# Folding batch 1's first DFT in four slabs, and moving the stage that fills the wait before the last DFT

## The chip, the cores and the metric

The kernel runs on one core of a Trainium2 chip. The metric is the device time of one execution, in microseconds (us). Engines are named as in the profile: PE is TensorE (PEld its weight loads), DVE VectorE, ACT ScalarE, POOL GpSimd, SP SyncE, which here issues most of the DMAs.

## The reference

```python
def _attn_ref(x, filt_r, filt_i):              # x: (8, 3008, 256) f32
    X = np.fft.rfft(x, axis=1)
    Y = X * (filt_r + 1j * filt_i)[None, :, :]
    return np.fft.irfft(Y, n=x.shape[1], axis=1)

def _moe_ref(x, w_gate, w_val, w_out):         # 24064 tokens, 256 -> 1536 -> 256
    gate = np.maximum(x @ w_gate, 0.0)
    return (gate * (x @ w_val)) @ w_out
```

A filter along the sequence through a real FFT of length 3008 for each of eight batches, then a gated MLP on all tokens.

## The kernel before

3008 is 94 x 32, so each batch goes through four steps of matmuls. **A** is the DFT over the 94 rows n1, in f32, one slab of columns at a time; its result goes to DRAM (Abuf) and comes back with other rows on the partitions. **B** is the transform over the 32 n2 (psX), the product with the filter (tt, uu), and its inverse (psD); **D** is what B leaves: it is copied out of PSUM into dsb by ACT and stored to DRAM (Dbuf). **C** reads it back (dC) and makes the inverse DFT over n1 (psY), which gives the MLP its input. The MLP is a loop of 47 blocks of 512 tokens with 12 steps each (psV, psG, then psO of the block before). Batch 0's A, B and first C stand ahead of the loop. Batches 1 to 7 are mixed inside it, but batch 1's A doesn't fit there: it must be back from DRAM by step 16 or so of the loop, and its x must be there early. So it stands ahead of the loop too, partly inside batch 0's B, partly in the wait for D's way through DRAM to C.

The parts that matter, from the kernel before (cuts are marked with `...`):

```python
def load_x(b, eng, cols):                   # x in pieces of 32 rows, on every 4th partition of all 128
    for c, c0, c1 in cols:
        for m in range(3):
            rows = min(32, B * N1 - (b * N1 + 32 * m))
            eng.dma_start(XF[c][m:m + 4 * rows - 3:4, c0:c1],
                          _ap(x, (b * N1 + 32 * m) * N2 * D + c * w + c0, [[N2 * D, rows], [1, c1 - c0]]))

def items_a(b):                             # A: 16 f32 matmuls of 128 x 96 over 512 columns
        ...
        nc.tensor.matmul(psA[0:NROW], WA, XF[c * NC2 // NX2][:, o:o + 512], start=True, stop=True)
        nc.scalar.copy(st["asb"][:NROW, j * 512:(j + 1) * 512], psA[0:NROW])
        ...                                 # after every fourth: store to Abuf

def first_b(amid):                          # batch 0's B
    for i in range(6):
        fwd(0, i)                           # psX
        if i > 1:
            inv(0, i - 2, cuts=cuts)        # psD, its copies to dsb, the store
        ...                                 # filter products on DVE, some on GpSimd
        amid(i)                             # from the third on: one or two of batch 1's A
    inv(0, 4, cuts=cuts); amid(6); inv(0, 5, cuts=cuts)
...
load_x(1, nc.sync, ((0, 0, 2 * q), (0, 2 * q, 4 * q), (1, 0, 4 * q)))
load_vg(0, DFF // 2)                        # half of the V and G weights
first_b(amid)
load_d(0, 0, 2)                             # dC <- Dbuf, for C
for c in range(2, 4):
    load_vg(c * DFF // 4, (c + 1) * DFF // 4)
load_at(1, 0)
for i, f in enumerate(early):               # the rest of batch 1's A, ten matmuls
    f()
    if i == 5: load_at(1, 1)
    if i == 7:
        for h in range(2): item_c(0, h)     # C of the first block; the last two of A stand behind it
...                                         # the loop; load_at(1, 2), load_at(1, 3) in its first two steps
```

## Time and profile before

| | before |
|---|---|
| median of the first three runs | 902.18 us (902.16 to 902.97) |
| span of the profiled run | 895.9 us |
| TensorE busy | 98% |
| first forward product of batch 0 (psX) | 35.12 us |
| load of C's data issued (D has landed) | 54.70 us |
| C | 58.56 us |
| first MLP matmul (psV) | 60.80 us |
| batch 1's first forward product | 79.67 us, no wait before it |

The prediction shows the page's busy line, the windows by stage, the chain that ended last and TensorE's timeline around C, and how they are read. TensorE's timeline around batch 1's first forward product (start and length in us, engine, line, operation, output and inputs, shapes; a bracket at the end would name a wait):

```profile
79.05 0.60 PE L486 MATMUL psO<-WoT,prod 128*128 128x256 bf16 x4
79.67 0.41 PE L364 MATMUL psX<-at,F 64*64 64x256 bf16 x8
80.02 0.61 PE L467 MATMUL psV<-yT,WvT 128*128 128x512 bf16 x2
```

In the text below, times are often given **after psX0**, the first forward product of batch 0 in that same run, because the stages ahead of it, which the change hardly touches, vary by up to 2 us from run to run. D's landing is read from the moment at which SP issues the first load of C's data, since that issue waits for D's last store.

### The profile page before, as it was taken

What the parts mean: (1) busy time and instruction counts of PE and PEld (TensorE: products, weight loads), DVE (VectorE), ACT (ScalarE), POOL (GpSimd) and SP (SyncE); (2) the same over time, 40 slices, a digit from 0 to 9 for tenths busy, and PEclk for the clock granted to TensorE, in tenths of its full rate; (3) what the DMA queues carried; (4) which work ended last, traced back from release to release, by engine and by line L of the source; (5) the groups of instructions that cost most, each with busy time, mean ns of one, the idle gap of its engine ahead of it and who ended that gap; (6) DMA issues with size and microseconds to landing.
All of it is one profiled execution on the core that took longest, in us unless ns stands there. A gap on an engine that the chain in (4) does not pass through costs nothing.

```text
span 895.9 us, 19186 instructions
## 1 busy us (share of the span) xinstructions
PE 881.8 (98%) x7206; PEld 510.3 (57%) x7206; DVE 569.3 (64%) x873; ACT 499.4 (56%) x891; POOL 363.6 (41%) x361
## 2 busy tenths in 40 slices
PE   7899999999999999999999999999999999999998
PEld 2335555566556665556655666555655566666665
DVE  2636865577665776567766677657766577655553
ACT  3475565556555556555655565555565556555553
POOL 4351399138661376415672167801868000000001
PEclk9999999999999999999999999999999999999999
DMA  9998448534465435463375433763346512241111
GB/s 247 287 230 168 108 141 185 124 82 116 124 155 130 115 104 137 129 139 98 99 176 130 99 101 105 181 133 85 111 139 154 117 32 82 67 88 36 37 30 54
DMA packets 114098, 109.17 MB, mean 122 GB/s; under 512 B 20359, under 2 KB 98599, under 8 KB 113366
## 3 DMA queue, kind: packets, MB, share of 16 engines
q1 hardware_dynamic: 90294, 80.10, 34.6%
q0 software_dynamic: 22992, 26.41, 12.4%
q10 hardware_dynamic: 720, 1.45, 0.4%
q8 instruction: 56, 0.92, 0.4%
q14 instruction: 36, 0.29, 0.1%
HBM read 61.93 MB, written 49.81 MB: 125 GB/s over the span
## 4 chain that ended last, share of the span: by engine, by line
PE 84%; POOL 6%; issue 4%; DMA 3%; DVE 1%; ACT 1%; SPq 0%; POOLq 0%; DVEq 0%
PE psV L467 25%; PE psO L486 25%; PE psG L467 24%; PE psF L323 3%; PE psY L451 2%; PE psD L394 2%; PE psX L364 1%; DMA Fti<-in_filt_i_dram 1%; POOL XP L296 1%; POOL fold L309 1%; POOL XP L310 1%; POOL XP L605 1%; DMA Dbuf<-dsb 1%; PE psJ L520 1%; POOL XP L300 1%
## 5 line engine op out<-in xcount | busy, mean ns | idle before, releaser
L472 DVE SCALAR_TENSOR_TENSOR prod<-psG,vsb 128x512 bf16<-128x512 f32 x564 | 389.2, 690 | 265.9 <-ACT vsb L470 259.1
L470 ACT CAST vsb<-psV 128x512 bf16<-128x512 f32 x564 | 332.1, 589 | 266.1 <-PE psV L467 226.9
L467 PE MATMUL psV<-yT,WvT 128*128 128x512 bf16 x1128 | 336.4, 379 | 0.3 <-ACT vsb L470 0.3
L486 PE MATMUL psO<-WoT,prod 128*128 128x256 bf16 x2256 | 336.4, 273 | 0.0
L467 PE MATMUL psG<-yT,WgT 128*128 128x512 bf16 x1128 | 335.3, 379 | 0.8 <-ACT dsb L401 0.3
L486 PEld LDWEIGHTS <-prod 128*128 128x128 bf16 x2256 | 220.6, 98 | 143.4
L467 PEld LDWEIGHTS <-WgT 128*128 128x128 bf16 x1128 | 110.0, 98 | 135.8 <-issue 2.4
L467 PEld LDWEIGHTS <-WvT 128*128 128x128 bf16 x1128 | 98.4, 98 | 42.1 <-issue 30.8
L258 POOL CAST scr<-yT 128x8 f32<-128x8 bf16 x25 | 4.7, 190 | 263.4 <-ACT yT L456 263.4
L509 POOL DMA_DIRECT2D out_dram<-osb x5 | 2.6, 536 | 196.1 <-ACT osb L499 196.1
L380 DVE TENSOR_TENSOR tt<-psX,Ftr 128x512 bf16<-128x512 f32 x96 | 65.1, 683 | 7.4 <-PE psX L364 7.4
L499 ACT COPY osb<-psO 128x512 f32<-128x512 f32 x92 | 53.9, 586 | 27.4 <-PE psO L486 25.7
L309 POOL TENSOR_TENSOR fold<-XP 128x1024 f32<-128x1024 f32 x24 | 56.5, 2355 | 21.5 <-PE psF L323 20.4
L380 DVE TENSOR_TENSOR uu<-psX,Fti 128x512 bf16<-128x512 f32 x89 | 60.6, 681 | 0.0
L401 ACT CAST dsb<-psD 128x512 bf16<-128x512 f32 x96 | 51.5, 589 | 12.4 <-PE psD L394 12.2
L296 POOL DMA_DIRECT2D XP<-in_x_dram x96 | 56.7, 596 | 1.6 <-issue 0.8
L310 POOL TENSOR_TENSOR XP<-XP 128x1024 f32<-128x1024 f32 x24 | 56.3, 2348 | 1.9
L330 DVE CAST asb<-psF 128x512 bf16<-128x512 f32 x48 | 30.9, 686 | 19.2 <-PE psF L323 14.1
L330 ACT CAST asb<-psF 128x512 bf16<-128x512 f32 x48 | 25.8, 589 | 29.0 <-PE psF L323 29.0
L456 ACT CAST yT<-psY 128x512 bf16<-128x512 f32 x47 | 27.6, 586 | 24.9 <-PE psY L451 24.7
L458 DVE CAST yT<-psY 128x512 bf16<-128x512 f32 x47 | 32.0, 681 | 9.7 <-PE psY L451 9.7
L451 PE MATMUL psY<-M,dC 96*128 96x94 bf16 (+18 forms) x604 | 37.5, 198 | 0.5 <-DMA dC<-Dbuf 0.4
(69 smaller groups left out, 508.2 us busy)
## 6 DMA issues: line engine op xcount, KB each, us to landing
at<-Abuf SPq DMA_DIRECT2D x32, 384.0 KB
dC<-Dbuf SPq DMA_DIRECT2D x64, 192.0 KB
XP<-in_x_dram POOLq DMA_DIRECT2D x48, 256.0 KB, 6.0
Dbuf<-dsb SPq DMA_DIRECT2D x23, 512.0 KB
XP<-in_x_dram POOLq DMA_DIRECT2D x96, 96.0 KB, 2.7
Abuf<-asb SPq DMA_DIRECT2D x96, 96.0 KB
out_dram<-osb SPq DMA_DIRECT2D x69, 94.0 KB
XF<-in_x_dram SPq DMA_DIRECT2D x15, 256.0 KB
```

The lines of the kernel that those rows point to most:

```text
L296: nc.gpsimd.dma_start(xp[r:r + 24, 0:4:2, :], _ap(x, (b * N1 * N2 + o) * D, [[N2 * D, 24], [47 * N2 * D, 2], [1, 512]]))
L309: tt(t, xp[:, 0:2], xp[:, 2:4], op=ALU.add)
L310: tt(xp[:, 2:4], xp[:, 0:2], xp[:, 2:4], op=ALU.subtract)
L330: copy(asf[:, :, q, :], banks[q])
L380: nc.vector.tensor_tensor(p, psX, filt, op=ALU.mult)
L401: nc.scalar.copy(dsb[:, a, o:o + 2, :], psD[a])
L451: nc.tensor.matmul(psY[:, o:o + w], dCs[b, n2 // 8][:, n2 % 8, h * 128:(h + 1) * 128], M1[:, n1:n1 + w], start=True, stop=True)
L467: nc.tensor.matmul(pt[:, :W], w[:, h, ft * 128:(ft + 1) * 128], yt[:, h, :], start=(h == 0), stop=(h == 1))
L470: nc.scalar.copy(vsb, psV[:, :W])
L472: nc.vector.scalar_tensor_tensor(prod, in0=psG[:, :W], scalar=0.0, in1=vsb, op0=ALU.max, op1=ALU.mult)
L486: nc.tensor.matmul(psO[:, t % 2], prods[ft][:, t * 128:(t + 1) * 128], WoT[:, ft, :], start=(ft == 0), stop=(ft == NFT - 1))
L499: copy(osb[:, t0 % 2:t % 2 + 1], psO[:, t0 % 2:t % 2 + 1])
```

## The change

The intent is to shorten the first B and to bring C forward. Batch 1's A leaves the first B. It is done with half the multiplications: the rows n1 and n1 + 47 are first added and subtracted (`fold_half`), and then 64 x 64 tiles do four products at a time (in the kernel before, one f32 matmul of 512 columns takes 0.86). Two slabs of it fill the wait for C, with junk matmuls (their results are never read) between them, meant to keep TensorE's clock up (it was 0.59 and 0.55 from 40 to 44 us in the kernel before); the third follows C, and the fourth goes into the loop at step 4. For these tiles, two on each half of the partitions, x is loaded in pieces that each lie in one half of the partitions. D's last piece gets a buffer of its own, the banks of psX and psD are fixed, and of the V and G weights one quarter, not two, is asked for ahead of the first B.

The core of the diff, cut at `...`:

```diff
+    def load_halves(c):
+        for t in range(3):
+            for h in range(2):
+                nc.sync.dma_start(X1[c][64 * h + t:64 * h + t + 61:4],
+                                  _ap(x, ((N1 + 16 * t) * N2 + 16 * h + 8 * c) * D,
+                                      [[N2 * D, 16], [47 * N2 * D, 2], [1, 8 * D]]))
+    def fold_half(j, eng):
...
+        eng.tensor_tensor(t, xp[:, 0], xp[:, 1], op=ALU.add)
+        eng.tensor_tensor(xp[:, 1], xp[:, 0], xp[:, 1], op=ALU.subtract)
+    def halves_a(j):
...
+        for q in range(2):
+            for h in range(2):
+                for e in range(2):
+                    nc.tensor.matmul(banks[2 * h + q][64 * e:64 * e + 64],
+                                     W1[64 * h:64 * h + 64, 64 * e:64 * e + 64], fold[1, j][e][...],
+                                     start=True, stop=True, tile_position=(64 * h, 64 * e))
...                                          # copies to asb; every second slab: eight stores to Abuf
-    def fwd(b, i):
+    def fwd(b, i, junks=False):
...
+            for _ in range(2 * junks):
+                nc.tensor.matmul(psXs[b, i, e], junk[:, 0:128], junk, start=True, stop=True)
...
-            dsbs[b] = i, sb.tile([128, 2, 4, D], BF16, tag="dsb", bufs=3, name="dsb")
+            pool, bufs = (sb, 3) if b or i < 5 else (pro, 1)
+            dsbs[b] = i, pool.tile([128, 2, 4, D], BF16, tag="dsb", bufs=bufs, name="dsb")
...
-    load_x(1, nc.sync, ((0, 0, 2 * q), (0, 2 * q, 4 * q), (1, 0, 4 * q)))
+    for c in range(2):
+        load_halves(c)
-    load_vg(0, DFF // 2)
-    first_b(amid)
+    load_vg(0, DFF // 4)
+    first_b()
     load_d(0, 0, 2)
+    for j in range(3):
+        fold_half(j, nc.vector)
-    for c in range(2, 4):
+    for c in range(1, 4):
         load_vg(c * DFF // 4, (c + 1) * DFF // 4)
-    load_at(1, 0)
-    for i, f in enumerate(early):
...
+    fold_half(3, nc.gpsimd)
     load_o()
+    warm(6)
+    for j in range(2):
+        halves_a(j)
+        warm((4, 6)[j])
+    for h in range(2):
+        item_c(0, h)
+    halves_a(2)
...
         if b == 1:
-            for c in range(2, 4):
-                at_step(c - 2, lambda c=c: load_at(1, c))
+            at_step(4, lambda: halves_a(3))
+            for c in (0, 2, 1, 3):
+                at_step(4, lambda c=c: load_at(1, c))
```

More of the change, by code (lines that the diff above doesn't have):

```diff
@@ L105, in _tables @@
     fold = np.zeros((128, 4, 32))
+    half1 = np.zeros((128, 4, 32))
     i = np.arange(24)
@@ L115, in _tables @@
             fold[32 * q:32 * q + 24, 2 * odd + 1, 0:24] = np.where(k1 % 47 == 0, 0.0, -np.sin(th))
+        th = 2 * np.pi * (np.outer(np.arange(47) - 23, k1) % N1) / N1
+        for h in range(2):
+            n = np.arange(47)
+            rows = 64 * h + 4 * (n % 16) + n // 16
+            half1[rows, 2 * odd, 0:24] = np.cos(th)
+            half1[rows, 2 * odd + 1, 0:24] = np.where(k1 % 47 == 0, 0.0, -np.sin(th))
     tab = np.concatenate([perm, swap, own.reshape(128, -1), m1], 1)
-    return wa.astype(np.float32), fold.reshape(128, 128).astype(np.float32), f2.astype(NBF16), tab.astype(NBF16)
+    fold = np.stack([fold, half1], 1).reshape(128, 256)
+    return wa.astype(np.float32), fold.astype(np.float32), f2.astype(NBF16), tab.astype(NBF16)
 @with_exitstack
@@ L155 @@
     Dbuf = [dram.tile([NROW * N2, D], BF16, name=f"Dbuf{b}") for b in range(B)]
-    XF = [pro.tile([128, NX2 * D], FP32, name=f"XF{c}") for c in range(N2 // NX2)]
+    XF = [consts.tile([128, NX2 * D], FP32, name=f"XF{c}") for c in range(N2 // NX2)]
+    XD = [t[:, :].rearrange("p (k n) -> p k n", k=4) for t in XF]
+    XP = [XD[j // 2][:, :, 512 * (j % 2):512 * (j % 2) + 512] for j in range(4)]
     WA = pro.tile([128, NROW], FP32)
-    WF = consts.tile([128, 4, 32], FP32)
+    WFS = consts.tile([128, 2, 4, 32], FP32)
+    WF, W1 = WFS[:, 0], WFS[:, 1].rearrange("p c k -> p (c k)")
     M1 = consts.tile([NROW, N1], BF16)
@@ L182 @@
     FILT = ((filt_r, Ftr), (filt_i, Fti))
+    junk = pro.tile([128, 512], BF16, tag="junk", bufs=1)
     tabs = pro.tile([128, tab_h.shape[1]], BF16, tag="tabs", bufs=1)
@@ L261, with fft_tag @@
     turn = {"tags": ("fft", "psv", "psg", "pso"), "i": 0}
-    def fft_tag(side=False):
-        if side and turn.get("side"):
-            return turn["side"]
+    def fft_tag():
         turn["i"] += 1
@@ L273, in one @@
                 st["asb"] = sb.tile([128, NC2 * D], BF16, tag="asb", bufs=4, name="asb")
-            psA = ps.tile([128, 512], FP32, tag=fft_tag(True), name="psA")
+            psA = ps.tile([128, 512], FP32, tag=fft_tag(), name="psA")
             o = (c * NC2 % NX2) * D + j * 512
@@ L280, in one @@
             if j == 3:
-                eng = nc.scalar if b and c > 1 else nc.sync
-                eng.dma_start(_ap(Abuf[b], c * NROW * NC2 * D, [[NC2 * D, NROW], [1, NC2 * D]]),
+                nc.sync.dma_start(_ap(Abuf[b], c * NROW * NC2 * D, [[NC2 * D, NROW], [1, NC2 * D]]),
                                   st["asb"][:NROW])
@@ L306, in fold_chunk @@
         xp = XP[j]
-        t = fs.tile([128, 2, 512], FP32, tag="fold", bufs=2, name="fold")
+        t = sb.tile([128, 2, 512], FP32, tag="fold", bufs=2, name="fold")
         tt = nc.gpsimd.tensor_tensor
@@ L325, in tiled_a, with store_a @@
                                  tile_position=(r, 32 * c))
+        store_a(b, j, banks, (nc.scalar.copy, nc.vector.tensor_copy) * 2)
+    def store_a(b, j, banks, copies):
         asf = sb.tile([128, NC2 * D], BF16, tag="asb", bufs=4, name="asb")
@@ L328, in tiled_a @@
         for q in range(4):
-            copy = nc.scalar.copy if q % 2 == 0 else nc.vector.tensor_copy
-            copy(asf[:, :, q, :], banks[q])
+            copies[q](asf[:, :, q, :], banks[q])
         for c in range(4):
@@ L342, in load_at_tiled @@
                                   [[D, 32], [N2 * D, 24], [1, D]]))
-    POOL_U = ((0, 1), (1, 0), (1, 1), (2, 0), (2, 1), (3, 1), (4, 0))
+    X1 = [t[:, :].rearrange("p (k n) -> p k n", k=2) for t in XF]
+    slabs = {}
+    def load_halves(c):
[4 more added lines that the diff above has]
+                                      [[N2 * D, 16], [47 * N2 * D, 2], [1, 8 * D]]))
@@ new lines, in fold_half @@
+    def fold_half(j, eng):
+        xp = X1[j // 2][:, :, 4 * D * (j % 2):4 * D * (j % 2) + 4 * D]
+        pool, tag = (pro, "half") if j < 2 else (sb, "fold")
+        t = pool.tile([128, 2, 2 * D], FP32, tag=tag, bufs=2, name="half")
+        t = t.rearrange("p q n -> p (q n)")
+        eng.tensor_tensor(t, xp[:, 0], xp[:, 1], op=ALU.add)
+        eng.tensor_tensor(xp[:, 1], xp[:, 0], xp[:, 1], op=ALU.subtract)
+        fold[1, j] = (t, xp[:, 1])
+    def halves_a(j):
+        banks = [ps.tile([128, 2 * D], FP32, tag=t, name="psF") for t in ("psv", "psg", "fft", "fft")]
+        c, m = divmod(j, 2)
+        for q in range(2):
+            for h in range(2):
+                for e in range(2):
+                    nc.tensor.matmul(banks[2 * h + q][64 * e:64 * e + 64],
+                                     W1[64 * h:64 * h + 64, 64 * e:64 * e + 64],
+                                     fold[1, j][e][64 * h:64 * h + 64, 2 * D * q:2 * D * q + 2 * D],
+                                     start=True, stop=True, tile_position=(64 * h, 64 * e))
+        copies = (nc.scalar.copy,) * 4 if j < 3 else (nc.scalar.copy, nc.vector.tensor_copy) * 2
+        for h in range(2):
+            if m == 0:
+                slabs[h] = sb.tile([128, NC2 * D], BF16, tag="asb", bufs=4, name="asb")
+            for q in range(2):
+                o = (4 * m + 2 * q) * D
+                copies[2 * h + q](slabs[h][:, o:o + 2 * D], banks[2 * h + q])
+            if m == 1:
+                for t in range(4):
+                    r = 2 - 2 * (t // 2) + t % 2
+                    nc.sync.dma_start(_ap(Abuf[1], ((2 * h + c) * NROW + r) * NC2 * D,
+                                          [[4 * NC2 * D, 24], [1, NC2 * D]]),
+                                      slabs[h][32 * t:32 * t + 24])
@@ L345 @@
+    POOL_U = ((0, 1), (1, 0), (1, 1), (2, 1), (3, 0), (3, 1), (4, 0))
     ats = {}
@@ L354 @@
     CUTS = (0, 2, 4, 6)
-    def fwd(b, i):
+    def fwd(b, i, junks=False):
         for e in range(2):
-            psXs[b, i, e] = ps.tile([128, 2, D], FP32, tag=fft_tag(), name="psX")
+            tag = "fft" if b or not e else "psv"
+            psXs[b, i, e] = ps.tile([128, 2, D], FP32, tag=tag, name="psX")
+            for _ in range(2 * junks):
+                nc.tensor.matmul(psXs[b, i, e], junk[:, 0:128], junk, start=True, stop=True)
         for m in range(2):
@@ L381, in product, with inv @@
         tus[b, i, e, k] = p
-    def inv(b, i, tags=None, cuts=CUTS):
+    def inv(b, i, tags, cuts=CUTS):
         if i in cuts:
-            dsbs[b] = i, sb.tile([128, 2, 4, D], BF16, tag="dsb", bufs=3, name="dsb")
+            pool, bufs = (sb, 3) if b or i < 5 else (pro, 1)
+            dsbs[b] = i, pool.tile([128, 2, 4, D], BF16, tag="dsb", bufs=bufs, name="dsb")
         i0, dsb = dsbs[b]
-        psD = [ps.tile([128, 2, D], FP32, tag=tags[a] if tags else fft_tag(), name="psD")
+        psD = [ps.tile([128, 2, D], FP32, tag=tags[a], name="psD")
                for a in range(2)]
@@ L404, in inv, with first_b @@
                               dsb[:, :, :o + 2, :])
-    def first_b(amid):
-        cuts = (0, 2, 4, 5, 6)
+    def first_b():
+        cuts, tags = (0, 2, 4, 5, 6), ("psg", "pso")
         for i in range(6):
-            fwd(0, i)
+            fwd(0, i, True)
             if i > 1:
-                inv(0, i - 2, cuts=cuts)
+                inv(0, i - 2, tags, cuts)
             for e in range(2):
@@ L415, in first_b @@
                 product(0, i, e, 1, pool=(i, e) in POOL_U)
-            amid(i)
-        inv(0, 4, cuts=cuts)
-        amid(6)
-        inv(0, 5, cuts=cuts)
+        for i in range(4, 6):
+            inv(0, i, tags, cuts)
     dCs = {}
@@ L511, in o_part @@
                                           osb[o + c0:o + c1, tt % 2])
-    junk = pro.tile([128, 512], BF16, tag="junk", bufs=1)
     def warm(n, cols=512):
-        psJ = ps.tile([128, 512], FP32, tag=fft_tag(True), name="psJ")
+        psJ = ps.tile([128, 512], FP32, tag=fft_tag(), name="psJ")
         for i in range(n):
@@ L535 @@
     load_x(0, nc.sync, ((0, 0, q), (0, q, 2 * q), (0, 2 * q, 4 * q), (1, 0, 2 * q), (1, 2 * q, 4 * q)))
-    nc.sync.dma_start(WF, nc.inline_tensor(fold_h, name="dft_fold").ap())
+    nc.sync.dma_start(WFS, nc.inline_tensor(fold_h, name="dft_fold").ap())
     for (src, dst) in FILT:
@@ L566 @@
         warm(2)
-    load_x(1, nc.sync, ((0, 0, 2 * q), (0, 2 * q, 4 * q), (1, 0, 4 * q)))
-    early = items_a(1)
-    def amid(i):
-        if i < 2:
-            warm(4, 256)
-        else:
-            for _ in range((1, 1, 2, 1, 1)[i - 2]):
-                next(early)()
+    for c in range(2):
+        load_halves(c)
     hold_gpsimd(ats[0][0:32, NG - 1, 0:8])
-    load_vg(0, DFF // 2)
-    turn["tags"], turn["side"] = ("fft", "psv", "psg"), "pso"
-    first_b(amid)
-    turn["tags"], turn["side"] = ("fft", "psv", "psg", "pso"), None
+    load_vg(0, DFF // 4)
+    first_b()
     load_d(0, 0, 2)
+    for j in range(3):
+        fold_half(j, nc.vector)
     nc.gpsimd.dma_start(pro.tile([1, D], BF16, tag="last", bufs=1, name="last"),
                         _ap(Dbuf[0], (N2 * NROW - 1) * D, [[D, 1], [1, D]]))
-    for c in range(2, 4):
+    for c in range(1, 4):
         load_vg(c * DFF // 4, (c + 1) * DFF // 4)
-    load_at(1, 0)
-    for i, f in enumerate(early):
-        f()
-        if i == 5:
-            load_at(1, 1)
-        if i == 7:
-            for h in range(2):
-                item_c(0, h)
-    hold_gpsimd(yTs[0][:, 0, 0:8])
-    load_o()
+    fold_half(3, nc.gpsimd)
+    load_o()
+    warm(6)
+    for j in range(2):
+        halves_a(j)
+        warm((4, 6)[j])
+    for h in range(2):
+        item_c(0, h)
+    halves_a(2)
     prologue.close()
     fs = ctx.enter_context(tc.tile_pool(name="fs", bufs=2))
-    XP = []
-    def clear_chunks():
-        for i in range(4):
-            XP.append(fs.tile([128, 4, 512], FP32, tag=f"XP{i}", bufs=1, name=f"XP{i}"))
-            nc.gpsimd.memset(XP[i], 0.0)
     turn["tags"] = ("fft",)
@@ L615 @@
     C_AT = (8, 10)
-    at_step(2, clear_chunks)
     for b in range(1, B):
```

## The prediction

> **What bounds the kernel now.** I read the page's busy table first, then the windows by stage, the chain that ended last around the start, and TensorE's timeline. Columns of a window: length, then busy time (and instructions) of PE, PEld, DVE, ACT, POOL, then granted clock, DMA share, GB/s.
>
> ```profile
> PE 881.8 (98%) x7206; PEld 510.3 (57%) x7206; DVE 569.3 (64%) x873; ACT 499.4 (56%) x891; POOL 363.6 (41%) x361
> ```
> ```profile
> 28.00:62.00 34.00, 31.27 (x231) 13.10 (x230) 15.21 (x27) 19.94 (x37) 15.39 (x19) 0.95 0.87 249
> 62.00:74.00 12.00, 11.43 (x62) 5.13 (x60) 8.80 (x13) 7.90 (x14) 6.48 (x4) 1.00 1.18 250
> ...
> 160.00:270.00 110.00, 110.00 (x963) 64.19 (x939) 73.53 (x113) 63.14 (x114) 54.62 (x52) 1.00 0.48 122
> ```
> From 160 us on TensorE has no gap, and the change touches nothing in its order there: batches 2 to 7 still fold and transform as before. So the change can act only between the first transform (35.1 us) and batch 1's first forward product (79.67 us). All else is a constant, and the question is by how much that second point moves.
>
> ```profile
> 42.88 0.96 ACT dsb L401 x2
> ...
> 51.16 1.07 ACT dsb L401 x2
> 52.24 0.03 ACT asb L279
> 52.26 2.42 DMA Dbuf<-dsb
> 54.68 0.02 issue
> 54.70 0.33 SPq L427
> 55.02 0.05 issue
> 55.08 3.35 DMA dC<-Dbuf
> 58.42 0.14 issue
> 58.56 0.62 PE psY L451 x12
> 59.18 1.80 PE psA L276 x4
> ```
> ```profile
> 49.42 1.10 PE L276 MATMUL psA<-XF,WA 128*96 128x512 f32 x2
> ...
> 51.01 7.11 PE L276 MATMUL psA<-XF,WA 128*96 128x512 f32 x16
> 58.56 0.62 PE L451 MATMUL psY<-M,dC 96*128 96x94 bf16 x12 [0.43 <-DMA dC<-Dbuf]
> 59.02 1.94 PE L276 MATMUL psA<-XF,WA 128*96 128x512 f32 x4
> 60.80 0.59 PE L467 MATMUL psV<-yT,WvT 128*128 128x512 bf16 x2
> ```
> The reader is to see two chains of nearly the same length: the last copy out of D (52.23) through the store, the load and C (6.33 us from copy to C), and TensorE's own A of batch 1, which fills that wait down to 0.43 us. Each f32 matmul of 512 columns is two records, 0.86 us together (7.11 us for eight matmuls with their drain). The loop starts at 60.80.
>
> ```profile
> 40.00:42.00 2.00, 2.00 (x16) 0.43 (x16) 0.09 (x1) 2.00 (x5) 2.00 (x3) 0.59 1.08 350
> 42.00:44.00 2.00, 2.00 (x18) 0.98 (x15) 1.79 (x3) 1.52 (x4) 1.79 (x2) 0.55 1.14 407
> ```
> Here TensorE has a little over half its clock, right after 34 to 40 us, in which it idled 2.3 us.
>
> [...] 16 f32 matmuls of 24x32 over 512 columns take 1.07 us in the chain, where one alone streams 0.86. [...]
>
> **The change part by part.**
> Removed: sixteen f32 matmuls of A, 16 x 0.86 = 13.8 us of TensorE, six of them inside the first B. Each also had an ACT copy of 0.58. GpSimd's four memsets (7.1 us) go; they lay beside the loop.
> Added: A as four slabs of eight 64x64 tiles. Four tiles run at once, so a slab is 2 x 0.86 + about 0.25 fill = 2.0 us, 8.0 us in all. Junk matmuls: 24 in the first B and 16 in three warm groups, 0.213 each, 8.5 us. TensorE's sum hardly changes; what matters is where it falls.
>
> First B. Before it ran 35.1 to 51.05, since A's matmuls (at half clock at first) stood between its steps. I list the new order with the old durations: DVE product pitch 0.60, ACT copy pitch 0.5 to 0.59, GpSimd product 1.13, eight psX matmuls 0.41, sixteen psD 0.5, four junk 0.85. GpSimd's first product still ends at 39.31, which starts the first inverse; the third GpSimd product frees the second inverse at 41.6; transform 4 is ready 43.35, transform 5 at 45.2; GpSimd's seventh product ends about 47.2, DVE's last 47.75. The last inverse ends about 48.35, and ACT's last copy 49.85: 2.4 us earlier than 52.23. The separate buffer for the last piece only keeps this free: before, the first store had landed at 48.42, well ahead of the last copy (51.16).
>
> D to C. With the same 6.33 us, the data for C are there at 56.2. TensorE comes later, though. DVE's first fold can only start after its last product[...]. Slab 0 then runs to 52.2. The next warm group takes a bank that ACT's third copy of the slab frees at about 53.3, so slab 1 runs 54.15 to 56.1 and six junk matmuls end at 57.4. C runs at 57.4 (58.56 before), a gain of 1.2. After C stands a slab of 2.0 where 1.80 stood, so the loop starts at about 60.0, a gain of 0.8. Its first steps wait for ACT and DVE some 0.6 us as before (0.28 and 0.3 are named in the waits).
>
> In the loop. Slab 3 stands after step 4. TensorE has no slack there (block 0 runs a step in 0.866, four pairs of 0.216), so it costs its 2.0 us in full, and about 0.1 for bank turns. From loop start to batch 1's first transform it was 79.67 - 60.80 = 18.87; it becomes 21.0. So that transform comes at 60.0 + 21.0 = 81.0, against 79.67: 1.3 us later.
>
> Transfers. The quarters of V and G leave the queue free during the first B, but three of them follow D instead of two. From 52 us on some 6.6 MB have to move before 81 us (dC 0.8 + 0.8, weights 1.2 + 0.8, A's store 1.5 and load 1.5); at the 250 GB/s of the windows that is 26.4 us, ending about 79 to 80. A's load follows slab 3's store, so it is just in time; I allow 0 to 1 us.
> Sum on the path: -1.2 (C earlier) + 0.2 (slab 2) + 2.1 (slab 3 in the loop) + 0.2 (transfers) = +1.3, so 903.5.
>
> **The rivals.**
> First: C is bound by its data, not by my warm groups. That a warm group stands just ahead of C speaks for it: whoever placed it seems to have seen TensorE wait there. If fold and banks cost less than I reckon, C runs at 56.2, and the sum is about +0.1. If the first B is also 1 us shorter[...], -1: 901 to 902.
> Second: batch 1's load or the weights come late. The DMA share above 1.1 in 62 to 74 us speaks for it[...]. TensorE would stand still for 1 to 3 us: 904.5 to 906.
> Third: TensorE falls to half clock again in the first B or between the slabs, some 3 us of it: +1 to +1.5. [...]
> Fourth: a loss of everything, a tie at 902, if gain and slab 3 cancel.
>
> **Range and chances.** My steps say 903.5; the first rival, which the placing of the warm groups supports, pulls to 901.5. I weigh them six to four and take 902.7. The range 900.0 to 905.5 holds both and a stall of some 2 us. Two per cent are 18 us, more than the whole stage between first B and loop could give: faster 0.01, same 0.98, slower 0.01.
>
> **What would show it.** Last copy out of D near 49.9; [...] slabs of 2.0 us on TensorE; C at 56.2 to 57.5; first psV near 60; batch 1's first psX near 81 with little wait on its load; from there to the end the same length as before. It is wrong if slabs don't run four tiles at once (3.5 us each), if C comes before 55, or if TensorE waits over 2 us in the loop.

Measured in the kernel after, the folds took 1.21 to 1.23 us each. For three other figures: the junk matmuls of the kernel before stand 0.216 us apart (30 in 6.64 us, the last of them 0.38 long) for the 0.213 reckoned with; the 1.07 us of 16 f32 matmuls of 24x32 is that of their 32 records in the chain, at 240.48 us for one; and the clock of the kernel before is 0.50 in each half microsecond from 40.5 to 43.5 us, and some 3 us of this is what the third rival means by "again".

## The result, and the profile after

The changed kernel took 901.82 us in the median of four runs (901.12 to 904.52); the kernel before, on the same occasion, 902.17 (901.29 to 902.97). The ratio is 1.0002, with a 95% interval from 0.9978 to 1.0026: the same. Ratios in this document are the mean time of one kernel's fast runs over that of the other's fast runs of the same rounds, so not quite the ratio of the medians that are quoted. The outputs of both kernels, and of every experiment below, are correct.

The page's busy line of the kernel after (busy time, share of the span, instructions):

```profile
PE 876.7 (97%) x7146; PEld 510.7 (57%) x7270; DVE 577.7 (64%) x881; ACT 498.0 (55%) x889; POOL 363.6 (40%) x360
```

Its windows by stage, with the columns that the prediction explains:

```profile
28.00:62.00 34.00, 29.33 (x276) 12.16 (x278) 23.34 (x34) 17.28 (x33) 15.71 (x18) 1.00 0.92 232
62.00:74.00 12.00, 11.44 (x63) 4.72 (x64) 7.43 (x12) 8.72 (x16) 5.01 (x4) 1.00 1.23 231
...
160.00:270.00 110.00, 109.10 (x924) 64.59 (x939) 72.74 (x112) 62.47 (x112) 60.86 (x57) 1.00 0.49 126
```

The late stage is as before. In the stage from 28 to 62 us the clock is whole (1.00 where it was 0.95), the DMA engines are busier (0.92 for 0.87), and yet they move less (232 GB/s for 249). The chain of work that ended last, in the kernel after (start, length, what):

```profile
49.64 1.10 ACT dsb L463 x2
50.76 4.49 DMA Dbuf<-dsb
...
55.76 3.40 DMA dC<-Dbuf
...
59.29 0.62 PE psY L511 x12
59.91 1.88 PE psF L384 x16
...
71.21 4.65 DMA Abuf<-asb
...
75.92 7.17 DMA at<-Abuf
83.10 2.29 issue
85.39 0.41 PE psX L425 x8
```

Two things are new in it. D's last store takes 4.49 us, where it took 2.42 before. And the way of batch 1's A through DRAM (its store, its load at<-Abuf) now ends the idle time before psX; before, psX stood behind plain MLP work. TensorE's timeline at the same places:

```profile
57.13 1.47 PE L578 MATMUL psJ<-junk 128*128 128x512 bf16 x6
59.29 0.62 PE L511 MATMUL psY<-M,dC 96*128 96x94 bf16 x12 [0.69 <-DMA dC<-Dbuf]
61.73 0.60 PE L527 MATMUL psV<-yT,WvT 128*128 128x512 bf16 x2
85.39 0.41 PE L425 MATMUL psX<-at,F 64*64 64x256 bf16 x8 [2.79 <-issue]
```

The brackets show that C waited 0.69 us for its data, in spite of the junk ahead of it, and that psX of batch 1 stood still for 2.79 us. For this second wait the profile names no releaser: "issue" is time for which it shows no cause. One piece of batch 1's load is seen to land at 83.10, 2.29 us before psX starts. That the rest of the wait is for the load's other pieces is inferred: the share of the DMA engines was 1.20 from 84.0 to 84.5 us and 0.39 from 85.25 to 85.5, so they ran empty just as psX began. Below, "the wait for batch 1's load" is meant in this sense. Right behind that idle time two windows of the kernel after lie at a little over half clock (the seventh value behind the length, 0.57 and 0.58):

```profile
86.00:88.00 2.00, 2.00 (x9) 1.06 (x8) 1.29 (x3) 0.59 (x1) 0.00 (x0) 0.57 0.04 11
88.00:90.00 2.00, 2.00 (x8) 0.89 (x7) 0.73 (x2) 1.17 (x2) 0.00 (x0) 0.58 0.04 10
```

The timelines of ACT and DVE in the kernel after show the end of the first B and the folds:

```profile
47.54 3.20 ACT L463 CAST dsb<-psD 128x512 bf16<-128x512 f32 x6 [0.96 <-PE psD L456]
48.59 1.21 DVE L373 TENSOR_TENSOR half<-XF 128x1024 f32<-128x1024 f32 x1
49.84 1.23 DVE L374 TENSOR_TENSOR XF<-XF 128x1024 f32<-128x1024 f32 x1
```

The last copy out of D ends at 50.74 us, which is 14.7 after psX0 (52.23 - 35.12 = 17.1 before). So the first B did become 2.4 us shorter. D, however, landed no earlier. The milestones in us after psX0, from one profiled run each; the last but one column is TensorE's wait right before batch 1's first psX:

| run | D landed | C | loop starts | batch 1's psX | wait there | span |
|---|---|---|---|---|---|---|
| before | 19.6 | 23.4 | 25.7 | 44.6 | 0 | 895.9 |
| before, again | 19.1 | 23.1 | 25.3 | 44.1 | 0 | 896.7 |
| after | 19.3 | 23.2 | 25.7 | 49.3 | 2.8 | 902.7 |
| after, again | 18.7 | 23.2 | 25.6 | 48.2 | 1.8 | 900.3 |
| after, a third time | 19.5 | 23.4 | 25.9 | 48.1 | 1.4 | 899.5 |

From batch 1's psX to the end it is 816.2 us before and 817.3 after, of which about 2 are the half clock just shown (an estimate: 4 us at 0.57 and 0.58); in the repeated runs it is 816.6 for before and 816.6 and 816.2 for after. So nearly everything happens where the prediction placed it, between psX0 and batch 1's psX.

### The profile page after: what moved, and what is told of

Its sections match the earlier page's. It is cut to its first block, busy times and chain, and to the rows that moved or that the text cites. A ratio compares the mean times of both kernels' runs of the same rounds, so it can differ in the third digit from the quotient of the medians.

```text
span 902.7 us, 19221 instructions
## 1 busy us (share of the span) xinstructions
PE 876.7 (97%) x7146; PEld 510.7 (57%) x7270; DVE 577.7 (64%) x881; ACT 498.0 (55%) x889; POOL 363.6 (40%) x360
## 4 chain that ended last, share of the span: by engine, by line
PE 85%; DVE 4%; ACT 3%; DMA 3%; issue 2%; SPq 1%; POOL 1%; ACTq 0%; POOLq 0%
PE psG L527 26%; PE psO L546 25%; PE psV L527 24%; DVE prod L532 4%; PE psF L332 3%; ACT vsb L530 3%; PE psD L456 2%; PE psX L425 2%; PE psY L511 1%; DMA XF<-in_x_dram 1%; SPq L187 1%; PE psJ L578 1%; POOL uu L439 1%; DMA at<-Abuf 1%; DMA Abuf<-asb 1%
## 5 line engine op out<-in xcount | busy, mean ns | idle before, releaser
L527 PE MATMUL psG<-yT,WgT 128*128 128x512 bf16 x1106 | 331.4, 380 | 6.4 <-ACT dsb L463 0.6
L527 PE MATMUL psV<-yT,WvT 128*128 128x512 bf16 x1030 | 315.7, 380 | 0.4 <-ACT vsb L530 0.3
L318 POOL TENSOR_TENSOR fold<-XF 128x1024 f32<-128x1024 f32 x24 | 56.5, 2355 | 22.0 <-PE psF L332 20.9
L305 POOL DMA_DIRECT2D XF<-in_x_dram x96 | 57.7, 604 | 0.9 <-issue 0.4
L319 POOL TENSOR_TENSOR XF<-XF 128x1024 f32<-128x1024 f32 x24 | 56.3, 2347 | 2.0
L511 PEld LDWEIGHTS <-dC 96*128 96x128 bf16 x604 | 34.4, 97 | 4.1 <-DMA dC<-Dbuf 1.2
```

Source lines behind the costliest of these rows:

```text
L305: nc.gpsimd.dma_start(xp[r:r + 24, 0:4:2, :], _ap(x, (b * N1 * N2 + o) * D, [[N2 * D, 24], [47 * N2 * D, 2], [1, 512]]))
L318: tt(t, xp[:, 0:2], xp[:, 2:4], op=ALU.add)
L319: tt(xp[:, 2:4], xp[:, 0:2], xp[:, 2:4], op=ALU.subtract)
L511: nc.tensor.matmul(psY[:, o:o + w], dCs[b, n2 // 8][:, n2 % 8, h * 128:(h + 1) * 128], M1[:, n1:n1 + w], start=True, stop=True)
L527: nc.tensor.matmul(pt[:, :W], w[:, h, ft * 128:(ft + 1) * 128], yt[:, h, :], start=(h == 0), stop=(h == 1))
```

## The experiments

Twelve runs were made, in four groups on three chips; each group has its own runs of the kernel before. The theories are these. **The queue**: D lands when the transfers asked for ahead of it are through, and batch 1's x now passes more slowly (244 GB/s from 36 to 48 us, for 311 before); so neither a shorter B nor TensorE's order sets C. Its rival, the prediction's: the junk groups and slabs ahead of C set C. And for the late load of batch 1: the **bytes** ahead of it (three quarters of V and G) against **asking too late** (slab 3 stands at step 4).

**Both kernels again** (b_again is the kernel before, a_again and a_third the changed one; no edit).

> The kernel before once more, unchanged, to learn how much one kernel varies. Ratio to itself 1.000. If the first profile (span 895.9 us) was typical, its span is 895 to 897 again and batch 1's first transform comes near 79.7 us. If it was a lucky one, as the 901 to 903 us of its timed runs suggest, the span is 899 to 901, and the profile shows a wait or a half-clock stretch that the first one had not.

> The changed kernel once more, unchanged. Ratio 0.998 to 1.003. If the late load of batch 1 (TensorE idle 2.8 us at 82.6 us, then half clock for some 4 us) belongs to the kernel, it is there again, near 83 us; if it was an accident of the profiled run, batch 1's first transform comes near 81 us without a wait.

> The changed kernel a third time, unchanged, for its time beside before and its stages. Ratio 1.000 to 1.003; rate 36 to 48 us near 240 GB/s, D landed 19 us after the first transform, C at 23.2, batch 1's first transform 48 to 49.5 after it with a wait of 1.5 to 3 us.

Measured: b_again 899.91 us, ratio to before 0.9987 [0.9963, 1.0010]. The changed kernel 901.89, ratio 1.0015 [0.9984, 1.0045], and on another chip 901.51, ratio 1.0032 [1.0000, 1.0065]. With the first result there are three comparisons: 1.0002, 1.0015 and 1.0032. The change is a tie or a loss of up to 0.3%; single runs of one kernel spread by 8 to 11 us (898.76 to 906.43 before, 899.09 to 910.17 after), more than that.

Where this spread comes from can partly be read from the granted clock of each run. Over 44 runs of the kernel before, time and clock have a correlation of -0.81, and a clock lower by 0.001 goes with about 0.9 us, which is a thousandth of the time. Their mean clock is 0.9973. In 16 runs of the changed kernel it is 0.9988, and all but one have 0.998 or more. Among runs of 0.998 or more the means are 899.7 us before (24 runs) and 901.9 after (15 runs). Over all runs they are 900.6 and 902.4. So at about the same clock the changed kernel is 2.2 us slower, and 1.8 us over all runs; put to an equal mean clock with the 0.9 us above, it would be about 3 us (an estimate). A steadier clock gives part of the loss back. The pools are from different rounds and chips, so this is a reading.

**C with less in front of it: no_warm.** The three junk groups go.

```diff
-    warm(6)
     for j in range(2):
         halves_a(j)
-        warm((4, 6)[j])
```

> The changed kernel without the sixteen junk matmuls of its three warm groups (those in the first B stay). The prediction's step says that TensorE's own work bounds C, so C comes up to 1.2 us earlier. The traces say C waits 0.6 to 0.7 us for its data with the junk in place, so C comes when it came (23.2 us after the first transform), with a wait of 2 to 3 us ahead of it; if the clock falls to half after that wait, the loop's first steps take up to 2 us longer.

Measured: 903.5 us, ratio 1.0039 [1.0014, 1.0065]. C started 22.9 us after psX0, 0.3 earlier than with all of the junk (23.2). TensorE's waits in this run (what waited, for what, us in total, times, longest):

```profile
PE psY L511 <- DMA dC<-Dbuf: 2.8, 1, 2.8
PE psX L425 <- issue: 2.5, 1, 2.5
```

TensorE was ready for C 2.4 us sooner (22.9 - 2.8 = 20.1 for 23.2 - 0.7 = 22.5), and waited for its data all the longer (2.8 us for 0.7). C's data bind, not the work ahead of it; the prediction's order of the two was wrong. Without the junk C came 0.3 us sooner than in the two earlier profiles of the changed kernel and 0.6 sooner than in the third (23.4), and no more.

**The last piece of D without its own buffer: no_own_buf.**

```diff
-            pool, bufs = (sb, 3) if b or i < 5 else (pro, 1)
+            pool, bufs = sb, 3
```

> The changed kernel with the last piece of D in the shared buffers (three) instead of one of its own. Theory 1, the prediction's: the own buffer is free of any effect, because the first store out of D has landed before the last copy wants its buffer; last copy out of D again 14.7 us after the first transform (14.0 to 15.0), C at 23.0 to 23.5, ratio to the kernel before as the changed kernel's, 1.000 to 1.004. Rival: with x loading at 245 instead of 300 GB/s the first store lands later than in the kernel before, so the last two copies wait for it; then the last copy is at 15.5 or later, C at 24 or later, and the time 0.7 us or more above the changed kernel's, 1.002 to 1.006.

Measured: 903.34 us, ratio 1.0027 [1.0005, 1.0050], inside the span of the changed kernel's own three ratios. The timeline of ACT and the chain, both of this run:

```profile
52.20 1.07 ACT L463 CAST dsb<-psD 128x512 bf16<-128x512 f32 x2 [2.58 <-PE psF L384]
```
```profile
52.68 0.59 ACT dsb L463
...
53.29 2.42 DMA Dbuf<-dsb
...
56.23 3.32 DMA dC<-Dbuf
59.55 0.14 issue
59.69 0.62 PE psY L511 x12
```

The last two copies now stand still for 2.58 us, since the first store out of D had not freed their buffer (the bracket names PE's psF, which the profile saw last; nothing else than this buffer was changed). psX0 is at 35.91 here, so the last copy ends at 53.27 - 35.91 = 17.4, which is 2.7 later than in the changed kernel. The rival foresaw this; that the own buffer is free of effect on the copy, as the prediction had it, is refuted. The store, 2.7 us later, takes 2.42 us instead of 4.49 (3.86 and 4.68 in the repeated runs), and D lands at 19.9 against 19.3: only 0.6 later (0.4 to 1.2 against the three profiles). C runs at 23.8 against 23.2. **The last copy can move by 2.7 us, and D lands nearly when it did.** This points to the queue ahead of the long store; x_early below tests it.

**The load of x in halves, alone, in the kernel before: b_x_half.** Only the pieces of batch 1's x are cut much as in the changed kernel: 16 rows each (two of 14), in one half of the partitions. The bytes are within 2% the same, and everything else is before's. One thing more changes: before loads the first half of the columns first, so its first slab of A needs three pieces of 256 KB, while here it needs six.

```diff
-    load_x(1, nc.sync, ((0, 0, 2 * q), (0, 2 * q, 4 * q), (1, 0, 4 * q)))
+    for c in range(2):
+        for m in range(3):
+            rows = min(32, N1 - 32 * m)
+            for r0, r1 in ((0, 16), (16, rows)):
+                nc.sync.dma_start(XF[c][m + 4 * r0:m + 4 * r1 - 3:4, :],
+                                  _ap(x, (N1 + 32 * m + r0) * N2 * D + c * NX2 * D,
+                                      [[N2 * D, r1 - r0], [1, NX2 * D]]))
```

> The kernel before, with nothing changed but the pieces in which batch 1's x is loaded: twelve of 16 partitions in one half of SBUF, as the changed kernel has them, instead of nine of 32 partitions from end to end. [...] the rate from 36 to 48 us falls from 310 GB/s to some 240, and D lands later relative to the first transform (21 us instead of 19.3) since its stores stand behind the load; C and the loop come 1 to 2 us later; time 1.001 to 1.002 of before. Rival (the rate of the changed kernel is low for another reason, such as its order of TensorE or fewer bytes in flight): rate stays near 310 and D lands at 19.3.

Measured: 902.91 us, ratio 1.0052 [1.0027, 1.0078]. The time is no less than what the whole change costs, but it does not come from the rate alone, as shown below. The window from 36 to 48 us, when x is under way (last three values: clock, DMA share, GB/s), for the kernel before, for b_again, for the changed kernel and for b_x_half, in this order:

```profile
36.00:48.00 12.00, 10.61 (x118) 4.67 (x118) 8.11 (x14) 9.04 (x18) 8.95 (x9) 0.86 1.02 311
```
```profile
36.00:48.00 12.00, 9.87 (x124) 4.42 (x128) 8.09 (x14) 8.69 (x17) 9.15 (x10) 1.00 1.02 302
```
```profile
36.00:48.00 12.00, 9.88 (x135) 4.33 (x137) 9.86 (x17) 7.40 (x14) 9.46 (x10) 1.00 1.07 244
```
```profile
36.00:48.00 12.00, 9.15 (x76) 3.64 (x76) 6.16 (x10) 6.02 (x11) 7.26 (x8) 0.60 1.01 239
```

At the same full share of the DMA engines (as counted here it can pass 1), the pieces of one half bring 239 to 244 GB/s (251 and 247 in the repeated runs), the wide ones 302 to 311. The lower rate comes with the pieces; nothing else of the change is needed for it. What in the pieces lowers it is not shown: each lies in one half of the partitions, where before's take every fourth of all 128, and each has 16 rows instead of 32, and no run here separates the two.

D landed 22.0 us after psX0 in this run, 2.4 later than before, about as expected, but not by the expected way. The last copy out of D and the issue of C's load, which follows D's landing:

```profile
55.18 1.07 ACT L401 CAST dsb<-psD 128x512 bf16<-128x512 f32 x2
58.85 1.87 SPq L427 DMA_DIRECT2D dC<-Dbuf  x4
```

From the copy's end (56.25) to D's landing it is 2.6 us, for 2.5 before (54.70 - 52.23): the store did not queue behind x here. The copy itself came 2.3 later (19.4 after psX0 for 17.1). B was slow: TensorE waited 0.91 us for x ahead of its first psA, and its clock was 0.50 in each window of 2 us from 40 to 48 us. All six runs of b_x_half have clocks of only 0.992 to 0.996, where before's eleven of the same group have 0.996 to 0.999. So this run shows the lower rate and no more: neither that it delays D in the changed kernel, nor what it costs there.

**x in wide pieces in the changed kernel: x_wide, and x_wide_vg with before's order of the weights (by the edit of vg_half below).** This was to give the changed kernel its rate back, with the same folds.

```diff
-            for h in range(2):
-                nc.sync.dma_start(X1[c][64 * h + t:64 * h + t + 61:4],
-                                  _ap(x, ((N1 + 16 * t) * N2 + 16 * h + 8 * c) * D,
-                                      [[N2 * D, 16], [47 * N2 * D, 2], [1, 8 * D]]))
+            for k in range(2):
+                nc.sync.dma_start(X1[c][t:t + 125:4, k],
+                                  _ap(x, ((N1 + 16 * t + 47 * k) * N2 + 8 * c) * D,
+                                      [[16 * D, 2], [N2 * D, 16], [1, 8 * D]]))
```

> The changed kernel with batch 1's x loaded in twelve pieces of the same 256 KB, but each over 32 partitions from end to end (every fourth) and one half of n1, in place of 16 partitions of one half of SBUF and both halves of n1. Theory[...]: the load of the changed kernel moves at some 240 GB/s where that of before moved at 310[...]; then the rate from 36 to 48 us returns to 300 or more, the D stores no longer queue behind it, D lands 1 to 2 us earlier relative to the first transform (17.5 instead of 19.2), C 0.5 to 1 us earlier (until the junk ahead of it binds), and batch 1's load about 1 us earlier. Rival (burst): D lands late because its three last pieces leave within 2 us of each other; then the rate rises but D still lands at 19.2. Time 0.998 to 0.999 of the changed kernel.

> Both the wide pieces of x and half of V's and G's weights ahead of D. [...] D lands as early as before the change or earlier, and 0.4 MB less follow it: batch 1's load lands 1.5 to 3 us earlier than in the changed kernel, with a wait under 1 us; time 0.997 of the changed kernel, 0.998 of before.

Measured: 947.73 us, ratio 1.0534 [1.0508, 1.0560], and 951.44, ratio 1.0567 [1.0541, 1.0592]. No theory foresaw this. The window in which x_wide loads:

```profile
42.00:58.00 16.00, 7.03 (x105) 3.45 (x104) 5.23 (x9) 6.75 (x14) 4.54 (x4) 0.90 0.13 51
```

The share of 0.13, at 51 GB/s, is as much as 2 of 16 DMA engines at work all the time (0.125), where the changed kernel has 1.07 from 36 to 48 us. The source's pattern now begins with a dimension of 2, where the changed kernel's begins with 16. What makes the share so low was not isolated. These two runs thus answer nothing about the width of the pieces, and with wide pieces at a full DMA share the changed kernel remains untried.

**Part of x earlier: x_early.** Two of the twelve pieces are asked for ahead of batch 0's last loads, in a stage where the queue is nearly idle (66 GB/s from 32 to 34 us in the changed kernel).

```diff
-    def load_halves(c):
+    def load_halves(c, ts=range(3)):
...
             load_at(0, 1)
+    load_halves(0, (0,))
     for c in range(2, 4):
...
-    for c in range(2):
-        load_halves(c)
+    load_halves(0, (1, 2))
+    load_halves(1)
```

> The changed kernel with two of the twelve pieces of batch 1's x asked for before the last two loads of batch 0 (the engines move only 66 GB/s from 32 to 34 us). Theory (D lands late because x at 240 GB/s is ahead of its stores): 0.5 MB less in the crowd lets D land up to 2 us earlier relative to the first transform (17.3 to 18), C 0.8 us earlier or so, until the junk ahead of it binds; batch 1's load lands as much earlier as D did, with TensorE's wait about the same or smaller. The first transform itself may come up to 1 us later. Rival (burst of D's last pieces): D lands at 19 as before.

Measured: 902.24 us, ratio 1.0030 [1.0010, 1.0050]. The last copies out of D, the issue of C's load, and C:

```profile
47.53 3.19 ACT L463 CAST dsb<-psD 128x512 bf16<-128x512 f32 x6 [0.96 <-PE psD L456]
53.35 1.87 SPq L487 DMA_DIRECT2D dC<-Dbuf  x4
58.42 0.63 PE L511 MATMUL psY<-M,dC 96*128 96x94 bf16 x12
```

psX0 is at 36.05 here. D landed 17.3 us after it, 2.0 earlier than in the changed kernel (18.7 to 19.5 in its three profiles), though its last copy is at 14.7 as there. So the bytes of x ahead of the store held it, and the burst of D's pieces, which is unchanged here, did not. C then waited for nothing and ran at 22.4, right behind its junk: here at last the prediction's order holds, because the queue was relieved, and its C (57.4 - 35.1 = 22.3 after psX0) is met. But batch 1's psX came at 48.1, with a wait of 2.4 us for its load, so of the 0.9 us at C nothing reached the end.

**Before's weights: vg_half.** Half of V and G ahead of the first B, two quarters behind it.

```diff
-    load_vg(0, DFF // 4)
+    load_vg(0, DFF // 2)
     first_b()
...
-    for c in range(1, 4):
+    for c in range(2, 4):
```

> The changed kernel with half of V's and G's weights ahead of D again, a quarter each less after it. Theory 1 (the engines are full from D's landing until batch 1's load lands): 0.4 MB less behind D at 240 GB/s lets that load land 1.6 us earlier relative to D's landing, so TensorE's wait of 2 to 3 us shrinks by about as much; D itself lands up to 1.5 us later, since those bytes share the engines with x and D. Sum near nothing. Theory 2 (the load is late because it is asked for late): wait unchanged at 2 to 3 us, time longer by what D loses.

Measured: 904.77 us, ratio 1.0057 [1.0030, 1.0083]. TensorE's waits in this run:

```profile
PE psY L511 <- DMA dC<-Dbuf: 2.0, 1, 2.0
...
PE psX L425 <- issue: 0.4, 1, 0.4
```

The wait for batch 1's load shrinks to 0.4 us, but this is no proof of the theory of the bytes. D lands 1.0 later (20.3 after psX0) and C 1.3, so TensorE comes later to the place of the wait. Batch 1's psX itself came at 48.3, within the 48.1 to 49.3 of the changed kernel; only from D's landing on is its load faster than there, by 0.7 to 2.1 us. What is gained at one end is lost at the other. The ratio is above the changed kernel's three, though its interval overlaps theirs, which suggests that asking for the weights in quarters was a good part of the change; the one profiled run of vg_half (span 900.5) would not tell so.

**Slab 3 sooner: slab3_step1.** All four folds on DVE, and slab 3 with its stores and loads at step 1 instead of 4.

```diff
-    for j in range(3):
+    for j in range(4):
         fold_half(j, nc.vector)
...
-    fold_half(3, nc.gpsimd)
...
-            at_step(4, lambda: halves_a(3))
+            at_step(1, lambda: halves_a(3))
             for c in (0, 2, 1, 3):
-                at_step(4, lambda c=c: load_at(1, c))
+                at_step(1, lambda c=c: load_at(1, c))
```

> The changed kernel with A's fourth slab (and the load after it) at step 1 of the loop instead of step 4, its fold on DVE. Theory 1: batch 1's load is late because the DMA engines are full from D's landing on; then it lands near 83 us as before and the wait stays 2 to 3 us, time the same within 1 us. Theory 2: it is late because it is asked for late; then it lands 2.6 us earlier, the wait is gone, and the time falls by 2.5 us or more (0.997 of the changed kernel).

Measured: 902.92 us, ratio 1.0017 [0.9993, 1.0041], that is, the changed kernel's own. The profiled run does not decide: its data for C came 3 us late, as the chain of this run shows:

```profile
49.78 4.99 DMA Dbuf<-dsb
55.29 5.85 DMA dC<-Dbuf
61.27 0.62 PE psY L511 x12
61.90 3.57 PE psF L384 x16
```

The load of C's data took 5.85 us instead of 3.4, and the slab behind C ran at half speed (3.57 for 1.88 us; the clock was 0.50 from 62 to 64 us). The loop began 4.6 us later than in the changed kernel, so batch 1's load was asked for at the same time as there (74.0 us), and that psX hardly waited says nothing of the step. Asking earlier has no support from the time and isn't refuted either.

**The third slab ahead of C: third_before_c.** This undoes the change's placing of the third slab behind C (its copies, half on DVE here, are left out of the cut).

```diff
     for j in range(2):
         halves_a(j)
-        warm((4, 6)[j])
+        if j == 0:
+            warm(4)
+    halves_a(2)
     for h in range(2):
         item_c(0, h)
-    halves_a(2)
```

> The changed kernel with A's third slab ahead of C, in place of the six junk matmuls there (its copies half on DVE). Theory: C waits for its data (they came at 59.2 us, the junk ended at 58.6), so the slab is free there and the loop starts some 2.0 us earlier, 59.9 instead of 61.7; time 0.998 of the changed kernel, less if the load for batch 1 then is waited for longer. Rival (the prediction's step): TensorE's own work bounds C, then C comes 0.7 us later and only about 1.2 us are won.

Measured: 902.7 us, ratio 1.0021 [0.9998, 1.0043], the changed kernel's again. C ran at 24.2 after psX0, 0.8 to 1.1 later than in the changed kernel, and the loop began at 25.3, 0.3 to 0.6 earlier than in its three runs, not 2.0. The slab isn't free in the wait for C. It ran from 56.76 to about 60.1 us, 3.3 instead of 1.9, as it takes the banks of the slab before, whose copies occupy ACT until 59.0; the data for C were there at 58.1. Batch 1's psX came at 47.5, 0.6 to 1.9 earlier than in the changed kernel's profiles; the times do not show it. Where the slab stands makes no difference that these runs could tell.

No experiment beat the kernel before, and none pointed to a combination that would.

## Why the prediction was right or wrong

The **time** was right: 902.7 predicted, 901.82, 901.89 and 901.51 measured, with 0.98 on a tie. The **range** of 900.0 to 905.5 held all three. By its own steps:

- "The last inverse ends about 48.35, and ACT's last copy 49.85": right. From psX0 the last copy ends at 14.7 us, as the steps had it (49.85 - 35.12). Moving A out of the first B did shorten it by 2.4 us.
- "A slab is ... 2.0 us": right. The chain shows 1.88 for slab 2 and 1.93 for slab 3. The folds on DVE take 1.21 to 1.23 us each.
- "With the same 6.33 us, the data for C are there at 56.2": **this step failed.** From the last copy to C it was 59.29 - 50.74 = 8.55 us. The step took the store's way as fixed; the store took 4.49 instead of 2.42, because it stood behind x. This is shown by x_early (bytes taken out of the queue move D's landing by 2.0) and borne out by no_own_buf (a copy 2.7 us later moves it by 0.6). That x was still in the way because it came at 244 instead of about 305 GB/s is likely, for b_x_half shows that the pieces alone lower the rate, but not isolated: the copy also came 2.4 us sooner, and the changed kernel with wide pieces was never measured. So the 1.2 us of C became 0.2.
- "C runs at 57.4", because of folds and junk groups: right in its size and wrong as the binding order. TensorE's own work ahead of C ended at 58.60, 22.5 after psX0 for 22.3 foreseen, but no_warm shows that the data bind. The first rival was right that they do; its figure of 56.2 was wrong with the step above.
- "The separate buffer for the last piece only keeps this free": wrong. I took the landing of the first store from the kernel before, at its time and rate. In the new order the copy would wait 2.6 us without this buffer. It hardly matters for the time, since the queue takes the place of the wait.
- Slab 3 "costs its 2.0 us in full": right. From the loop's start to batch 1's psX it is 23.66 - 2.8 of waiting = 20.9 us in the first profile, for 21.0 predicted and 18.87 before. In the repeated runs it is 20.9 and 20.8.
- "+0.2 (transfers)": mis-sized, and the second rival came true in part: the wait for batch 1's load was 2.8, 1.8 and 1.4 us in the three profiles. (Its sum is also a little off: 26.4 us from 52 end at 78.4, not "about 79 to 80".) Whether the cause is the bytes behind D or that the load is asked for late stays open. In x_early D landed 2.0 sooner and the wait stayed at 2.4; in vg_half the wait shrank, but mostly because TensorE came later; slab3_step1 did not decide.

The sum from psX0 to batch 1's psX, before against after, in the first profiles: C -0.2 (predicted -1.2), slab 2 behind C +0.2 (+0.2), slab 3 +2.0 (+2.1), the late load +2.8 (+0.2), together +4.8 where +1.3 was said. In the five profiles of both kernels it is +3.6 to +5.2. The timed runs show less, 0.2 to 2.9 us by the three ratios. The clock does not explain this gap: the profiled runs of before have clocks of 0.997 and 0.998, those of the changed kernel 0.998, 1.000 and 0.999, so they differ by about as much as the pools do (0.9973 and 0.9988). What differs is that the two profiled runs of before took 897.7 and 899.4 us, below its mean of 900.6, while the three of the changed kernel took 904.5, 902.1 and 901.3, about its mean of 902.4. Where a typical run of the kernel before loses these 2 us no profile shows.

So that the time came out right is in part luck. The prediction was set on the first runs of before, 902.2, which the 44 later ones put at 900.6, and it added 0.5 us (the steps' 1.3, weighed with a rival whose C at 56.2 did not come); over all runs the change costs 1.8. A base 1.5 too high and a loss 1.3 too small nearly cancel. (On what chip those first runs were made is not recorded; the four runs of before beside the result had 902.17 again.) The path alone was reckoned 2.3 to 3.9 us too short by the profiles. That the junk matmuls give the changed kernel its steadier clock was not isolated: no_warm, whose clocks lie between 0.993 and 0.999, fits it, but b_again has the whole clock from 36 to 48 us too, with none of the new junk, and its psX of batch 1 came only 0.5 us earlier than in the first profile.

## What to carry to other kernels

Before work is taken off a chain that ends in a store, see what else is in that store's queue: here 2.4 us of compute were saved and the data arrived when they did before, until bytes were taken out of that queue (x_early). When a load is cut anew so that the compute suits better, compare GB/s at equal DMA share before and after, and the DMA share itself; in these runs one such cut, to pieces of 16 rows in one half of the partitions, cost a fifth of the rate (239 GB/s for 302 to 311, at a share of 1.01 for 1.02), and another, with a pattern that begins with a dimension of 2, brought the share down to 0.13. And compare kernels at their mean clock over many runs: one profiled run of each was off by more than the whole effect.
